# Grouping the block products of a pair by where their weights lie, in a fused attention and channel-mix kernel

## The chip, the cores and the metric

The kernel runs on one core of a Trainium2 chip. The metric is the device time of one execution in microseconds. The kernel before took 392.95 us (median of 3 runs, 392.79 to 394.13).

## What is computed

Input is float32 throughout: 4 sequences of 768 positions, 8 heads of 64. First comes a local attention: chunks of 32 queries see 16 keys to the left, their own 32, 8 to the right and 8 memory keys. Its output, 4 x 768 x 512, is the `x` of a channel mix:

```python
x_prev = concat([zeros, x[:, :-1]], axis=1)
xk = mu_k * x + (1 - mu_k) * x_prev
xr = mu_r * x + (1 - mu_r) * x_prev
k = maximum(xk @ w_k, 0)              # 512 x 1024
v = (k * k) @ w_v                     # 1024 x 512
out = sigmoid(xr @ w_r) * v           # 512 x 512
```

## The kernel before, in words

The 3072 positions are 12 units (u) of 256 positions, each of two tiles (t) of 128. The steps of the program are operations of a small planner (`Plan`), and each has a name:

- `qk{t}`, `vw{t}`: loads of a tile's queries and keys (672 KB) and of its values (512 KB), on SyncE's queue. From unit 4 on the qk loads have two buffers (`ring`); the vw loads have two from unit 3 on.
- `s{u}`: scores of a unit, 128 small matmuls into two PSUM banks (L514). `max`, `sub`, `exp`, `sum`, `norm` follow on VectorE and ScalarE.
- `t{t}`: transposes of a tile's probabilities (L594), copied out of PSUM by `bd{t}.0` and `.1`; `a{t}`: attention product of a tile, 32 small matmuls (L611).
- `g{u}.{c}`: gate block of a tile, 12 matmuls of 512 columns and the last halved (L1104), then `sig` on ScalarE.
- `h{u}.{n}`: hidden blocks. Up to unit 5 there are four a unit, each of 24 matmuls of 256 columns (L1128). `v{u}.{n}`: value blocks; from unit 3 on seven products of 12 matmuls each (`seven`, L1452, banks `pa`, `pb`, `pc`).

Every product of float32 operands is made of three matmuls on split operands (high x high, high x low, low x high). VectorE and ScalarE make these splits.

From unit 6 on two units form a pair (6 and 7, 8 and 9, 10 and 11), and the hidden layer of a pair is computed by `squares` (L883) with seven products in place of eight: products 1 to 7, each in two halves s, so 14 products (q, s) of 12 matmuls of 256 columns (L1060). `PRODUCTS` (L37) gives their order; products 1, 2 and 4 use weights of `w_k` as they are, the others use sums of weights ("forms"). The forms were made once by VectorE, stored to DRAM (`forms`, L803) and are loaded again for each pair into four places (L1026): places 0 and 1 are the second halves of the tiles `wk[0]` and `wk[1]`, places 2 and 3 those of `wv[0]` and `wv[1]` (L795). In the kernel before, product 7.s and 3.s use place s, 6.0 and 6.1 place 2, 5.0 and 5.1 place 3. A place is loaded when the product that used it has ended. The moving operands (b11, b21, b22, t1 to t4 in `with_x`, L939) lie in six places too: two in `xs` (the space of xh0 and xl0), four in `khl`; t1 to t4 are made in place, one from the other. Partial sums go to banks A, G and B for each half; B starts as a copy of A (`seed`), `keep` copies a bank to SBUF, `add` adds a bank to it, `relu` and `sq` end a quarter.

PSUM has eight banks: two for scores, two under the tag `tp` (transposes, attention products), four under `m`, which are given out in turn.

The order of the work: TensorE's is written out by hand in `te_order` (L241). From unit 3 on a unit runs as hidden, attention products, gate, two value products, scores and transposes of a later unit, four value products, gate, last value product. At the end of unit 4 stand `a12 a13 v4.6 t14 t15 s8`, then the four hidden blocks of unit 5. In an even unit from 6 on the 14 products come first, the first gate block before the last of them, then two attention products. The order on the other engines and SyncE's queue is found by the planner: it walks through all operations with modelled costs, takes the one that can start first (`walk`, L140), where an operation with a late due time is put back by at most `WAIT`, and repeats that `PASSES` times with due times taken from the walk before. Each engine then runs its operations in that order.

Of the kernel before, what the change touches and what calls it, by code (L numbers as in the profile page):

```python
# [16 lines left out]
P = 128  # L17
# [17 lines left out]
FAST = 3  # L35
PAIR = 6
PRODUCTS = (  # L37
    (1, 0), (7, 0), (1, 1), (6, 0), (2, 0), (5, 0), (4, 0), (7, 1), (2, 1), (3, 0), (6, 1), (4, 1), (5, 1), (3, 1),
)
# [8 lines left out]
PART = 1.38  # L48
KEEP = ("big", "x4", "vw")
PASSES, WAIT, SLOPE = 40, 0.4, 0.1  # L50
FIRST = """
# [189 lines left out]
def te_order():  # L241
# [4 lines left out]
    for u in range(1, nu):  # L246
        a, b = 2 * u + 2, 2 * u + 3
        g = [("g", u + 1, c) for c in range(QPU) if u + 1 < FAST]
        h = [("h", u, f) for f in range(FT // 2)]
        v = [("v", u, n) for n in range(FT // 2)]  # L250
        x = [("a", a), ("a", b)]
        if u >= FAST:
            g = [("g", u, c) for c in range(QPU)]
            v = [("v", u, n) for n in range(7)]
            t = [("t", a + 2), ("t", b + 2)]
            near = u + 1 if u < PAIR - 1 else u + 2
            x = [("a", near * QPU + c) for c in range(QPU)]
# [36 lines left out]
def local_attention__then__channel_mix(  # L294
# [37 lines left out]
    def ps(tag, name, n=1):  # L332
        return psA.tile([P, n * 512], F32, tag=tag, name=name, bufs=bufs[tag])

# [318 lines left out]
    def mixed(deps):  # L653
        for m in (1, 0):
# [3 lines left out]
            def f_mix(m=m):  # L658
                x = T["xT", 0]
                for i in range(2):  # L660
                    T["xf", 0, m, i] = ps("m", f"xf{m}{i}")
                    for k in range(2 * i, 2 * i + 2):
# [220 lines left out]
    def squares(u0, u1):  # L883
# [38 lines left out]
        def less(name, to, x, y, deps):  # L922
# [15 lines left out]

# [22 lines left out]
        def bank(key, s):  # L961
            T[key, u0, s] = ps(slots[key, s].tag, f"{key}{u0}_{s}")

# [47 lines left out]
        for n, (q, s) in enumerate(PRODUCTS):  # L1011
            key = bank_of[q]
            deps, new, use = [prev], [], []
            if q in (1, 7):
                slots[key, s] = Slot("m" if s == 0 else "tp")
                new = [slots[key, s]]
            if q in direct:
                deps += wdeps(wk_hl, range(direct[q][0], direct[q][0] + 2))
            else:
                j = {7: s, 3: s, 6: 2, 5: 3}[q]  # L1020
                w = Slot(f"wf{j}")
# [9 lines left out]
                use.append(w)  # L1031
            if q == 3 and s == 0:
                operand("b22", "b22", ("x", 0), [mix[u1, 0, 3], t2])
            hh, ll, hs, ls = X[with_x[q]]
# [30 lines left out]
            prev = op(f"h{u0}.{n}", ("pe", PART), f, deps, new=new, use=use, due=due["h", u0, n])  # L1065
            if (q, s) == (5, 1):
                vparts["h"] = prev
            if q not in direct:
                users[j] = prev
            if q == 1:  # L1070
                slots["B", s] = Slot("m")

# [10 lines left out]
            elif q == 6:  # L1083
                done["keep", 5, s] = keep(u0, 2 + s, "B", s, prev)
            elif q == 2:
                relu(u0, s, "A", s, prev)
            elif q == 3:
                relu(u1, s, "B", s, prev)
            elif q == 4:
                add(u0, 2 + s, "G", s, [prev, done["keep", 5, s]])  # L1090
            elif q == 5:
                done["c22", s] = add(u1, 2 + s, "B", s, [prev, done["keep", 4, s]])
        hlast[u0] = hlast[u1] = prev

    def channel_mix(u):
# [45 lines left out]

        def bank(*key):
            T[key] = ps("m", "_".join(str(x) for x in key))

        first = u == 0
        gs = [Slot("m") for _ in range(QPU)]
        sgs = Slot("sg", [0] if u >= PAIR else None)
        xg, xgs = list(mix[u, 1][:2]), list(mix[u, 1][2:])  # L1150
        gdone, prev = [], None
        for n in range(QPU):
            def f_gate(n=n):
                if first:
                    for c in range(QPU):
                        if n == 0:
                            bank("pr", u, c)
                        gate(c, range(n * KT // 2, (n + 1) * KT // 2))
                else:
                    bank("pr", u, n)  # L1160
                    gate(n, range(KT))
# [34 lines left out]
        for n in range(FT // 2):  # L1196
            def f_hidden(n=n):
                if first:
                    for f in range(FT // 2):
                        if n == 0:  # L1200
                            bank("ph", u, f)
                        hidden(f, [n])
                else:
                    bank("ph", u, n)
                    hidden(n, range(KT))
# [54 lines left out]
        for n in range(FT // 2):  # L1260
# [3 lines left out]
            def f_value(n=n, c=c, half=half, fs=fs):  # L1264
                for c in range(QPU) if first else [c]:
                    if n == 0 if first else half == 0:
                        bank("pv", u, c)
                    value(c, fs)
# [26 lines left out]

    sums, free = {}, {}

# [80 lines left out]
    def seven(u, ks, o_g, sgs):  # L1378
# [11 lines left out]
        def operand(name, at, pair, deps):  # L1390
# [16 lines left out]
            ll = op(f"kl{u}.{name}", ("dve", 0.62, True), f_lo, [hh], new=[kl], use=use + [kh])  # L1407
            return hh, ll, kh, kl

# [16 lines left out]
        def bank(key):  # L1426
            T[key, u] = ps("m", f"{key}{u}")

# [70 lines left out]
        last = u == NU - 1  # L1499
        pa, pb, pc = Slot("m"), Slot("m"), Slot("m")  # L1500

# [54 lines left out]
    with tc.manual_schedule():  # L1556
        for o in plan.order(FIRST.split()):
            if o.eng == "pe":
                n = 0 if ("ph", 0, 0) in T else int((o.start - busy - 0.1) / (0.86 if busy else 1.72))
                for _ in range(n):  # L1560
                    warm = warm or ps("m", "warm")
                    nc.tensor.matmul(warm, zero, zeros, start=True, stop=True)
# [51 lines left out]
```

## Time and profile before

| | us |
|---|---|
| median of 3 runs | 392.95 |
| profiled execution | 393.63 |
| its span, first to last instruction | 391.9 |
| TensorE matmuls busy | 382.5 |
| TensorE weight loads busy | 352.9 |
| VectorE busy | 322.3 |
| ScalarE busy | 275.0 |
| GpSimd busy | 14.6 |
| data moved | 63.43 MB, 162 GB/s |

The granted TensorE clock is 1.00 in all forty slices of the span. In the chain of waits a line gives the start, the length and the work, merged (x12: twelve matmuls). Matmuls overlap by far more than their length of 280 ns tells, so the rate is read from the chain or from start to start, not from the busy time. "issue" is time in which an engine waited for nothing that the profile shows.

### The profile page before, as it was taken

To read this page: it belongs to the slowest core of one execution; us is meant where nothing else is said; L and a number is where in the kernel's file an instruction comes from. 1 tells how busy PE (TensorE), PEld (TensorE's weight loads), DVE (VectorE), ACT (ScalarE), POOL (GpSimd) and SP (SyncE) were. 2 spreads that over 40 slices of the span, in tenths; PEclk is the share of its full clock that TensorE was granted. 3 is DMA by queue.
4 is the path that set the end of the run, shared out by engine and by line. 5 is a ranking of instruction groups with operands and counts; after the bars stand their busy time and mean duration, and the time that the engine had idled before them with its cause. 6 is when DMAs were issued, how large, how long until landed. Compare 5 with 4: busy or idle time off the path is not lost.

```text
span 391.9 us, 11008 instructions
## 1 busy us (share of the span) xinstructions
PE 382.5 (98%) x4736; PEld 352.9 (90%) x4736; DVE 322.3 (82%) x540; ACT 275.0 (70%) x466; POOL 14.6 (4%) x14
## 2 busy tenths in 40 slices
PE   7799999999999999999899999999999999999996
PEld 3579889888988999999899999999999999999996
DVE  3699999888898999789979996799996598666673
ACT  3876795914795799488388597678877767496631
POOL 2221003010000000000000000000000000000000
PEclk9999999999999999999999999999999999999999
DMA  8999870411063246464837376735056601160011
GB/s 316 412 371 380 316 286 2 141 55 54 2 212 131 105 148 213 176 202 142 264 134 276 129 230 223 239 121 163 2 165 215 213 2 56 58 204 11 0 55 54
DMA packets 25344, 63.43 MB, mean 162 GB/s; under 512 B 2512, under 2 KB 9040, under 8 KB 24784
## 3 DMA queue, kind: packets, MB, share of 16 engines
q1 hardware_dynamic: 25296, 62.73, 45.4%
q8 instruction: 37, 0.61, 0.6%
q14 instruction: 11, 0.09, 0.1%
HBM read 52.24 MB, written 10.49 MB: 160 GB/s over the span
## 4 chain that ended last, share of the span: by engine, by line
PE 94%; ACT 2%; DVE 2%; DMA 1%; issue 0%
PE pr L1104 17%; PE ph L1128 17%; PE pc L1452 10%; PE pv L1104 8%; PE B L1060 7%; PE pa L1452 6%; PE pb L1452 6%; PE px L611 6%; PE G L1060 4%; PE A L1060 4%; PE s L514 4%; PE pt L594 3%; PE xf L665 2%; ACT k L399 1%; DMA qk<-in_qk_dram 1%
## 5 line engine op out<-in xcount | busy, mean ns | idle before, releaser
L1128 PE MATMUL ph<-xh,wkh 128*128 128x256 f32 x192 | 53.7, 280 | 1.0 <-issue 1.0
L1128 PE MATMUL ph<-xh,wkl 128*128 128x256 f32 x192 | 53.4, 278 | 0.0
L1128 PE MATMUL ph<-xl,wkh 128*128 128x256 f32 x192 | 53.3, 278 | 0.0
L1104 PE MATMUL pr<-wrh,xh 128*128 128x512 f32 x96 | 38.3, 399 | 0.0
L1403 DVE TENSOR_TENSOR khl<-k,khl 128x512 fp32r<-128x512 f32 x42 | 28.9, 688 | 10.7 <-ACT khl L369 10.5
L1104 PE MATMUL pr<-wrl,xh 128*128 128x512 f32 x96 | 37.6, 392 | 0.0
L1104 PE MATMUL pr<-wrh,xl 128*128 128x512 f32 (+1 forms) x117 | 37.6, 351 | 0.0
L1128 PEld LDWEIGHTS ph<-xh,wkh 128*128 128x128 f32 x192 | 36.2, 188 | 1.5 <-issue 1.2
L1128 PEld LDWEIGHTS ph<-xh,wkl 128*128 128x128 f32 x192 | 36.1, 188 | 0.0
L1128 PEld LDWEIGHTS ph<-xl,wkh 128*128 128x128 f32 x192 | 36.0, 188 | 0.0
L369 ACT CAST khl<-k 128x512 fp32r<-128x512 f32 x50 | 30.6, 618 | 3.5 <-DVE k L1413 3.1
L369 ACT COPY aTz<-pt 64x512 f32<-64x512 f32 x45 | 26.0, 580 | 8.0 <-PE pt L594 7.2
L1104 PE MATMUL pv<-wvh,khl 128*128 128x512 f32 (+1 forms) x97 | 30.3, 390 | 0.0
L1452 PE MATMUL pc<-wtbig,khl 128*128 128x256 f32 x216 | 28.2, 280 | 0.0
L1452 PE MATMUL pa<-wvh,khl 128*128 128x256 f32 x144 | 27.9, 279 | 0.0
L1452 PE MATMUL pb<-wtx,khl 128*128 128x256 f32 x216 | 27.5, 276 | 0.0
L611 PEld LDWEIGHTS px<-aTz,vw 128*64 128x64 f32 x768 | 23.4, 138 | 4.1 <-DVE aTz L371 2.6
L1223 ACT ACTIVATE k<-ph 128x512 f32<-128x512 f32 x24 | 14.1, 595 | 18.1 <-PE ph L1128 17.9
L611 PE MATMUL px<-aTz,vw 128*64 128x64 f32 x768 | 25.0, 224 | 1.6 <-DVE aTz L371 1.6
L1104 PEld LDWEIGHTS pr<-wrh,xl 128*128 128x128 f32 x117 | 22.0, 188 | 4.8
L1452 PEld LDWEIGHTS pc<-wtbig,khl 128*128 128x128 f32 x216 | 26.1, 188 | 0.0
L1452 PEld LDWEIGHTS pb<-wtx,khl 128*128 128x128 f32 x216 | 25.9, 188 | 0.0
(169 smaller groups left out, 1004.0 us busy)
## 6 DMA issues: line engine op xcount, KB each, us to landing
vw<-in_vw_dram SPq DMA_DIRECT2D x24, 512.0 KB, 5.4
ring<-in_qk_dram SPq DMA_DIRECT2D x16, 672.0 KB, 5.8
out_dram<-o SPq DMA_DIRECT2D x23, 256.0 KB, 2.1
qk<-in_qk_dram SPq DMA_DIRECT2D x8, 672.0 KB, 6.3
raw<-in_w_k_dram SPq DMA_DIRECT2D x4, 1024.0 KB, 7.8
raw<-in_w_v_dram SPq DMA_DIRECT2D x4, 1024.0 KB, 6.8
wvh<-forms SPq DMA_DIRECT2D x12, 256.0 KB, 3.1
wvl<-forms SPq DMA_DIRECT2D x12, 256.0 KB, 3.3
```

The source lines that it names most:

```text
L369: e.copy(dst, src)
L399: nc.scalar.activation(T["diag", m][:, j, k], id_sb, AF.Copy, scale=mu_sb[:, m + 2 * j, k : k + 1])
L514: nc.tensor.matmul(room(h, c)[CHUNK * j : CHUNK * (j + 1), r, :], q4[z, r, j, :], k3[z, r, STEP * j : STEP * j + NK], start=True, stop=True,)
L594: nc.tensor.transpose(p[:, n * P : (n + 1) * P], e[:, n // 2, c, n % 2, :], id_sb)
L611: nc.tensor.matmul(p3[64 * h : 64 * h + 64, 2 * g : 2 * g + 2, CHUNK * j : CHUNK * j + CHUNK], v[:, g, h, j, :], a[:, h, g, j, :], start=True,
L665: nc.tensor.matmul(z, T["diag", m][:, j, k], x[:, k, 1 - j : 1 - j + UTOK], start=j == 0, stop=j == 1)
L1060: nc.tensor.matmul(z, w, x[:, k], start=q in (1, 7) and i + k + m == 0, stop=i + k == 2 and m == 2, skip_group_check=q not in (1, 7),)
L1104: nc.tensor.matmul(p[:, a : a + step], x, w[:, a : a + step], start=start, stop=stop and a + step == DM)
L1128: nc.tensor.matmul(z, w, x[:, k], start=start, stop=stop)
L1223: e.activation(r, T["ph", u, f], AF.Relu)
L1403: nc.vector.tensor_sub(T["al", u, name], block(at), T["ah", u, name].bitcast(F32))
L1452: nc.tensor.matmul(p, l[:, i], r[i], start=start, stop=stop, skip_group_check=not fresh)
```

## The change

- `PRODUCTS` has a new order, by the tiles that hold the weights: (1, 0), (7, 0), (1, 1), (7, 1) in `wk[0]` and `wk[1]`; (2, s), (4, s) in `wk[2]` and `wk[3]`; (6, s) in places 2 and 3; (5, s) in places 0 and 1; (3, s) in places 2 and 3.
- In `te_order` the two attention products of units 6 and 8 stand on either side of the products 6, and the first gate block between the products 5 and 3. In unit 10, which has no attention, the gate block stands between 5.0 and 5.1, and the second gate block behind two value products.
- The transposes 14 and 15 and scores 8 move from the end of unit 4 into the hidden blocks of unit 5.
- The operands change places: b22 takes the `khl` place of t1 and is split before t2 is made; t2 overwrites b22's block; t4 is made from b21 and t2; t1 is split late, into b11's place. `add` for product 4's bank comes after product 6.
- In `seven` only a22 waits for the end of the pair's hidden products (all 14 now, before up to (5, 1)); the other operands wait for the last split of the same place.
- PSUM banks `m` get places: the planner picks the one that is free first (`KEEP`), and from unit 5 on most are fixed.
- The loads `qk{t}` and `vw{t}` from tile 12 on wait for a later step of TensorE. `WAIT` goes from 0.4 to 0.6, `SLOPE` from 0.1 to 0.15.

```diff
 PRODUCTS = (
-    (1, 0), (7, 0), (1, 1), (6, 0), (2, 0), (5, 0), (4, 0), (7, 1), (2, 1), (3, 0), (6, 1), (4, 1), (5, 1), (3, 1),
+    (1, 0), (7, 0), (1, 1), (7, 1), (2, 0), (2, 1), (4, 0), (4, 1), (6, 0), (6, 1), (5, 0), (5, 1), (3, 0), (3, 1),
 )
-KEEP = ("big", "x4", "vw")
-PASSES, WAIT, SLOPE = 40, 0.4, 0.1
+KEEP = ("big", "x4", "vw", "m")
+PASSES, WAIT, SLOPE = 40, 0.6, 0.15
...
+            if u == PAIR - 1:
+                h = h[:1] + extra[2:] + h[1:3] + extra[:2] + h[3:]
...
                 if u == PAIR - 2:
-                    seq += [("a", n + QPU) for _, n in x] + v[6:] + [("t", n + QPU) for _, n in t] + [("s", near + 3)]
+                    extra = [("t", n + QPU) for _, n in t] + [("s", near + 3)]
+                    seq += [("a", n + QPU) for _, n in x] + v[6:]
...
-                seq += h[:-1] + g[:1] + h[-1:] + x
                 if u == nu - 2:
-                    seq += g[1:] + v
+                    seq += h[:11] + g[:1] + h[11:] + v[:2] + g[1:] + v[2:]
                     continue
+                seq += h[:8] + x[:1] + h[8:10] + x[1:] + h[10:12] + g[:1] + h[12:]
...
+        pv = vparts[u0 - 1]
...
-        l21 = operand("b21", "b21", ("k", 0), [mix[u0, 0, 3], vparts[u0 - 1][5]])
-        lt1 = operand("t1", "b11", ("k", 2), [t1, vparts[u0 - 1][6], vparts[u0 - 1][3]])
-        t2 = less("t2", "b11", "b22", "b11", [lt1, t3])
-        operand("t2", "b11", ("k", 3), [t2, vparts[u0 - 1][3]])
-        t4 = less("t4", "b21", "b21", "b11", [t2, l21])
-        operand("t4", "b21", ("k", 1), [t4, vparts[u0 - 1][6]])
+        l21 = operand("b21", "b21", ("k", 0), [mix[u0, 0, 3], pv[5]])
+        l22 = operand("b22", "b22", ("k", 2), [mix[u1, 0, 3], pv[3], pv[6]])
+        t2 = less("t2", "b22", "b22", "b11", [l22, t3])
+        t4 = less("t4", "b21", "b21", "b22", [t2, l21])
+        operand("t4", "b21", ("k", 1), [t4, pv[6]])
+        operand("t2", "b22", ("k", 3), [t2, pv[3]])
...
-                slots[key, s] = Slot("m" if s == 0 else "tp")
+                slots[key, s] = Slot("tp") if q == 1 else Slot("m", [s])
...
-                j = {7: s, 3: s, 6: 2, 5: 3}[q]
+                j = s if q in (5, 7) else 2 + s
...
-                operand("b22", "b22", ("x", 0), [mix[u1, 0, 3], t2])
+            if q == 5 and s == 0:
+                operand("t1", "b11", ("x", 0), [t2])
...
-                slots["B", s] = Slot("m")
+                slots["B", s] = Slot("m", [3 - s])
...
-        gs = [Slot("m") for _ in range(QPU)]
+        gs = [Slot("m", None if u < PAIR else [int(u < NU - 2)] if n == 0 and (u - PAIR) % 2 == 0 else [3]) for n in range(QPU)]
...
-                free[u] = [vparts["h"]]
+                free[u] = [hlast[u]]
...
-            deps = deps + free.get(u, [])
+            if name == "a22":
+                deps = deps + free.get(u, [])
+            deps = deps + behind.get(pair, [])
...
-        pa, pb, pc = Slot("m"), Slot("m"), Slot("m")
+        pa, pb, pc = (Slot("m", [n] if u >= PAIR - 1 else None) for n in range(3))
...
+    line = sorted((o for o in plan.ops if o.alts[0][0] == "pe"), key=lambda o: o.due)
+    at = {o.name: n for n, o in enumerate(line)}
+    for o in plan.ops:
+        if o.name[:2] in ("qk", "vw") and int(o.name[2:]) // QPU > FAST + 2:
+            t = int(o.name[2:])
+            n = at[f"s{t // QPU - 1}"] + 5 if o.name[0] == "q" else at[f"a{t - 2}"] + 2
+            o.deps.append(line[n])
```

## Rows read from the trace of the kernel before

**Rows 1.** The page: busy time; instruction queue (packets, MB, share); engines of the chain.
```profile
PE 382.5 (98%) x4736; PEld 352.9 (90%) x4736; DVE 322.3 (82%) x540; ACT 275.0 (70%) x466; POOL 14.6 (4%) x14
...
q8 instruction: 37, 0.61, 0.6%
...
PE 94%; ACT 2%; DVE 2%; DMA 1%; issue 0%
```

**Rows 2.** TensorE's waits: engine, line, releaser; us in total, times, longest.
```profile
PE px L611 <- DVE aTz L371: 1.6, 2, 0.8
...
PE ph L1128 <- issue: 1.0, 1, 1.0
PE B L1060 <- DVE khl L915: 0.2, 1, 0.2
```

**Rows 3.** The chain in order of time, hidden blocks: start us, us, what.
```profile
125.64 11.09 PE ph L1128 x96
...
156.51 10.88 PE ph L1128 x96
...
190.26 1.42 PE s L514 x89
191.67 1.57 PE ph L1128 x12
193.25 1.00 issue
194.25 10.16 PE ph L1128 x84
```

**Rows 4.** The chain, pair of units 8 and 9.
```profile
283.96 1.36 PE A L1060 x12
...
288.04 1.42 PE B L1060 x12
...
302.08 2.73 PE pr L1104 x13
304.81 1.38 PE B L1060 x12
306.19 2.02 PE px L611 x64
308.20 1.58 PE pa L1452 x12
...
311.15 0.87 PE pt L594 x8
```

**Rows 5.** Windows on four value products, units 8 and 6, matmuls alone.
```profile
312.02:317.68 5.66, 5.66 (x48) 5.45 (x47) 1.00 0.07 27
254.60:260.07 5.47, 5.47 (x48) 5.27 (x47) 1.00 0.60 224
```

**Rows 6.** Windows: the pairs' stretches, products alone; the first number is the length.
```profile
283.96:309.78 25.82, 19.66 (x168) 19.38 (x167) 1.00 0.62 190
224.14:250.80 26.66, 20.23 (x168) 19.52 (x167) 1.00 0.66 212
339.09:361.31 22.22, 19.66 (x168) 19.38 (x167) 1.00 0.35 119
```

**Rows 7.** Timeline of unit 6: the second wait within its products.
```profile
241.38 0.30 PEld L1060 LDWEIGHTS B<-khl,wvh 128*128 128x128 f32 x2 [0.23 <-ACT k L369]
```

**Rows 8.** Timeline of SyncE's queue: the vw loads behind attention product 8.
```profile
137.86 1.69 SPq L587 DMA_DIRECT2D vw<-in_vw_dram  x2
```

**Rows 9.** The page's DMA issues: the last number is us from issue to landing.
```profile
ring<-in_qk_dram SPq DMA_DIRECT2D x16, 672.0 KB, 5.8
```

**Rows 10.** The page's costliest groups: VectorE's low part of a value operand.
```profile
L1403 DVE TENSOR_TENSOR khl<-k,khl 128x512 fp32r<-128x512 f32 x42 | 28.9, 688 | 10.7 <-ACT khl L369 10.5
```

**Rows 11.** Instructions on tile aTz: the copies of transposes, ns min/median/max.
```profile
L369 ACT COPY aTz<-pt x45: 558/580/587, 14.7 to 313.9; 64x512 f32<-64x512 f32 x45
```

**Rows 12.** Waits of SyncE's queue: the stored forms.
```profile
SPq L852 <- DVE ring L371: 12.0, 3, 4.8
```

More of the change, by code (lines that the diff above doesn't have):

```diff
@@ L332, in ps @@
     def ps(tag, name, n=1):
-        return psA.tile([P, n * 512], F32, tag=tag, name=name, bufs=bufs[tag])
+        if isinstance(tag, Slot):
+            tag = f"{tag.tag}at{tag.place}" if tag.tag == "m" else tag.tag
+        return psA.tile([P, n * 512], F32, tag=tag, name=name, bufs=bufs.get(tag, 1))
     id_sb = const.tile([P, P], F32, tag="ident", name="id_sb")
@@ L660, in f_mix @@
                 for i in range(2):
-                    T["xf", 0, m, i] = ps("m", f"xf{m}{i}")
+                    T["xf", 0, m, i] = ps(ss[i], f"xf{m}{i}")
                     for k in range(2 * i, 2 * i + 2):
@@ L961, in bank @@
         def bank(key, s):
-            T[key, u0, s] = ps(slots[key, s].tag, f"{key}{u0}_{s}")
+            T[key, u0, s] = ps(slots[key, s], f"{key}{u0}_{s}")
         def keep(u, f, key, s, dep):
@@ L1031, in squares @@
                 use.append(w)
-            if q == 3 and s == 0:
-                operand("b22", "b22", ("x", 0), [mix[u1, 0, 3], t2])
+            if q == 5 and s == 0:
+                operand("t1", "b11", ("x", 0), [t2])
             hh, ll, hs, ls = X[with_x[q]]
@@ L1065, in squares @@
             prev = op(f"h{u0}.{n}", ("pe", PART), f, deps, new=new, use=use, due=due["h", u0, n])
-            if (q, s) == (5, 1):
-                vparts["h"] = prev
             if q not in direct:
@@ L1084, in squares @@
                 done["keep", 5, s] = keep(u0, 2 + s, "B", s, prev)
+                add(u0, 2 + s, "G", s, [done["keep", 5, s], done["p4", s]])
             elif q == 2:
@@ L1089, in squares @@
             elif q == 4:
-                add(u0, 2 + s, "G", s, [prev, done["keep", 5, s]])
+                done["p4", s] = prev
             elif q == 5:
@@ L1140, in value, with bank @@
                         product(p, x[:, tc_], w, f + n == 0, stop, stop and c == QPU - 1 and u == 1)
-        def bank(*key):
-            T[key] = ps("m", "_".join(str(x) for x in key))
+        def bank(slot, *key):
+            T[key] = ps(slot, "_".join(str(x) for x in key))
         first = u == 0
-        gs = [Slot("m") for _ in range(QPU)]
+        gs = [Slot("m", None if u < PAIR else [int(u < NU - 2)] if n == 0 and (u - PAIR) % 2 == 0 else [3]) for n in range(QPU)]
         sgs = Slot("sg", [0] if u >= PAIR else None)
@@ L1156, in f_gate @@
                         if n == 0:
-                            bank("pr", u, c)
+                            bank(gs[c], "pr", u, c)
                         gate(c, range(n * KT // 2, (n + 1) * KT // 2))
                 else:
-                    bank("pr", u, n)
+                    bank(gs[n], "pr", u, n)
                     gate(n, range(KT))
@@ L1200, in f_hidden @@
                         if n == 0:
-                            bank("ph", u, f)
+                            bank(ms[f], "ph", u, f)
                         hidden(f, [n])
                 else:
-                    bank("ph", u, n)
+                    bank(ms[n], "ph", u, n)
                     hidden(n, range(KT))
@@ L1266, in f_value @@
                     if n == 0 if first else half == 0:
-                        bank("pv", u, c)
+                        bank(vs[c], "pv", u, c)
                     value(c, fs)
@@ L1294, in channel_mix @@
             op(f"out{u}.{c}", ("dma", 0.65), f_st, [o_o], use=[os], due=dv + BLOCK + 6)
-    sums, free = {}, {}
+    sums, free, behind = {}, {}, {}
     def quarter(s, kh, nh):
@@ L1403, in f_lo @@
                 nc.vector.tensor_sub(T["al", u, name], block(at), T["ah", u, name].bitcast(F32))
-            deps = deps + free.get(u, [])
+            if name == "a22":
+                deps = deps + free.get(u, [])
+            deps = deps + behind.get(pair, [])
             hh = op(f"kh{u}.{name}", either(act=(0.6,), dve=(0.36, True)), f_hi, deps, new=[kh], use=use)
             ll = op(f"kl{u}.{name}", ("dve", 0.62, True), f_lo, [hh], new=[kl], use=use + [kh])
+            behind[pair] = [ll]
             return hh, ll, kh, kl
@@ L1426, in bank @@
         def bank(key):
-            T[key, u] = ps("m", f"{key}{u}")
+            T[key, u] = ps({"pa": pa, "pb": pb, "pc": pc}[key], f"{key}{u}")
         def half(key):
@@ L1560, in local_attention__then__channel_mix @@
                 for _ in range(n):
-                    warm = warm or ps("m", "warm")
+                    warm = warm or ps("mat0", "warm")
                     nc.tensor.matmul(warm, zero, zeros, start=True, stop=True)
```

## The prediction

> **What bounds the kernel now.** I read the page first, then who waited for whom, then the chain of work in order of time, then windows on single stretches. The page says that TensorE is the limit: 98% busy and 94% of the chain that ended last [rows 1]. The list of TensorE's waits holds 6.0 us in all, most of it in the first 30 us, which the change doesn't touch; three of its lines matter here [rows 2]. So a gain must come from TensorE's own time: from a wait in mid-kernel, from the rate at which it takes matmuls, or from the price of switching between kinds of work. All three are seen in the chain.
>
> First, a hole. In unit 5 the four hidden blocks take 1.57 + 1.00 + 10.16 = 12.73 us, with 1.00 us in which TensorE waited for nothing that the profile shows; elsewhere four such blocks take 10.88 (units 2 to 4: 11.09 right behind a scores block) [rows 3]. The hole comes in the midst of a block, just behind a scores block, whose 128 matmuls and 128 weight loads run through in 1.42 us. The instruction queue moved 0.61 MB in 37 packets [rows 1]; over 2 x 4736 TensorE instructions that is 64 B each and 256 instructions a packet, so that one scores block uses up a whole packet in 1.42 us. I read the hole as code that came late. That is argued, since no view names it.
>
> Second, two rates. Twelve matmuls of 256 columns take 1.36 us or 1.41 us. In the pair of units 8 and 9 the first products take 1.36, the fourth 1.42 [rows 4], and the fourteen together 19.49 where 13 at 1.36 and the one behind the gate at 1.38 would make 19.06 (worked out below). It isn't the clock and isn't traffic: the same four value products took 5.66 us at a DMA share of 0.07 and 5.47 us at a share of 0.60, both at clock 1.00 [rows 5]. The slow rate begins where the stationary weights pass from the wk tiles to the wv tiles, and it stays until a gate block or a further such passage ends it; behind a gate block it was the fast rate each time.
>
> Third, attention products. Two in a row take 2.02 us, and the product behind them 1.58 in place of 1.36 [rows 4]: 1.01 us each, and 0.22 us for the turn.
>
> **The change, part by part.** The times are sums for the profiled execution (393.63 us, of them 391.9 us span).
>
> *Unit 5.* The transposes of tiles 14 and 15 and scores 8 go from in front of the hidden blocks to between them: block, scores 8, two blocks, transposes, block. The work is the same. The blocks are then 10.88 plus two restarts, each of 0.21 (11.09 against 10.88, rows 3): 11.30 us against 12.73, so **-1.43 us**, of which 1.00 is the hole. It should not come back behind scores 8, because now 24 matmuls stand before and 48 behind it, where two attention products, two transposes and the scores block came within six microseconds. If the last block runs at the slow rate, 0.1 of it is lost.
>
> *Pair of units 8 and 9.* New order: products 1.0, 7.0, 1.1, 7.1, 2.0, 2.1, 4.0, 4.1 (weights in wk), attention product, 6.0, 6.1 (wv), attention product, 5.0, 5.1 (wk), gate, 3.0, 3.1 (wv). Now every passage between wk and wv has other work in it. If that keeps the fast rate: 13 x 1.36 + 1.38 behind the gate = 19.06 us; gate 2.73; two single attention products, each 1.01 + 0.22, 2.46; the first value product 1.36. Sum 25.61 against 25.82 [rows 6]: **-0.21 us**. The rate alone gives 0.43 (the products were 25.82 - 2.73 - 2.02 - 1.58 = 19.49), and the second turn takes 0.22 back.
>
> *Pair 6 and 7.* The same stretch took 26.66 [rows 6], that is 0.84 more than the pair behind it. It waits 0.2 us for t2's low part (VectorE, rows 2) and 0.23 us for the copy of B on ScalarE [rows 7]; each wait also costs a restart. t2 is now wanted at the ninth product, not the fourth; the copy, which stood on ScalarE behind a relu that waits for the last stored forms, now comes before that relu. Both waits should go, and the forms are wanted no earlier, 7.1 excepted, whose place is free from the end of unit 5. What is late next is t4 at the seventh product, as late as before and then without a wait. 26.66 - 25.61 = **-1.05 us**.
>
> *Pair 10 and 11* has no attention, and 6.0 follows 4.1 directly: three products at 1.41 and, from 3.0 on, two more, so 21.79 + 0.25 = 22.04 against 22.22 [rows 6]: **-0.18 us** (between 0 and -0.43).
>
> These four give -2.87 us. Against them stand waits that before does not show:
>
> *Held-back loads.* From tile 12 on, a qk load waits for the fifth TensorE step behind the last scores, a vw load for the second step behind the attention product that freed its buffer; both were issued as soon as the buffer was free. Nothing else waits behind them but SyncE's queue (stores, forms). Tight is scores 6: its loads now start with the end of attention product 8, where SyncE issues the vw loads today [rows 8], and are wanted 6.7 us later (1.01 + 0.22 + 2.73 + 2 x 1.36), the second tile 0.7 after that. A qk load takes 5.8 us (median) [rows 9], the second is issued some 0.6 later. From 0 up to the issue of two vw loads that might go first, 1.7 us [rows 8]; a gain is out, since an earlier load never stopped TensorE. I take 0.1, nearest the median. All other held-back loads have over a microsecond to spare.
>
> *The operand a22* may be split only after product 3.1, no longer after 5.1, and s2 needs it. In unit 8 two value products and two transposes (1.36 + 1.36 + 0.87 = 3.59 us, rows 4) stand between; five VectorE passes at up to 0.69 [rows 10] make 3.45. From 0 to 1.2 (a longer VectorE pass that gets in between); I take 0.1.
>
> *Transposes 14 and 15* now lie one block (2.72 us) before their attention products: four copies of 0.58 on ScalarE [rows 11], 2.3 us. From 0 to 0.8, the longest such wait now [rows 2]: 0.05.
>
> *Restarts behind a single attention product* might land in the slow rate: two groups in each of two pairs, 0.1 each: from 0 to 0.4; I take 0.1. On the other side the four slow products of unit 8 [rows 5] may turn fast: down to -0.2, taken as nothing.
>
> *PSUM places* are fixed and loads on VectorE and ScalarE stay what they were: no instruction more. The gate's bank is wanted again 4 us behind it, its sigmoid takes 0.6: nothing.
>
> That is +0.35, and the net -2.5 us: 391.1 for the profiled execution. The three runs have a median of 392.95, 0.68 under it; the same step from there gives **390.4 us**.
>
> **The rivals.**
>
> *A. The hole is not in every execution, or moves behind another scores block.* For it: no view names its cause, and the three runs lie 1.34 us apart, about the hole and its restart. Against it: it stands where code is used fastest. Then 1.2 of the 1.43 is not won: 391.6 us.
>
> *B. Places don't matter.* The slow rate is something into which any restart can fall, and the new passages keep it: the products stay at 19.49, and the second turn of attention costs its 0.22 for nothing. For it: 5.66 and 5.47 us for the same operands [rows 5]; against it: all three pairs slow down at the same product. 0.43 + 0.43 + 0.18 less won: 391.4 us. The Trainium skill is on this side: "TensorE: Matmul & The Clock Gate" (Step-by-step) says that loading the next weights takes no read bandwidth from the running matmul; by that rule, where the two lie can't cost anything, and no row here shows it as a rule.
>
> *C. Slower: held-back loads come late.* The mechanism is SyncE's in-order queue. The loads for scores 9 may be issued only at the end of unit 5's last hidden block, 7.7 us before they are wanted (two attention products with their turn, a gate, two value products), at the moment that also frees the first form loads. If a stored form stands in front of them and waits for VectorE (one did for up to 4.8 us [rows 12]), the 1.7 us that they have to spare (7.7 less 5.8 and the issue) are used up and 3.1 missing, with up to 1.7 more at scores 6: 390.4 + 4.8 = 395.2 us. It decides from 2.5 us of late loading on. Against it: their buffers leave them the rest of the time idle, and the due times put a load that is wanted next in front.
>
> **How the numbers follow.** Forecast 0.55 (389.5 to 391.4, with its unknown costs at either end), A 0.18, B 0.12, C 0.15. What this kernel's runs can tell from no change is about 0.5%, 2 us: under 391.0 or over 394.9. Under 391.0 lie three quarters of the forecast and a sixth of A and B: 0.46. Over 394.9 lie two thirds of C: 0.10. The rest, 0.44, is between. With A and B inside, and outside two thirds of C and what of the forecast's unknown costs comes out better than their lower ends, the range is 389.4 to 394.2.
>
> **What would show it.** Right: no idle microsecond in unit 5, and its four blocks at some 11.3 us; the first eight products of each pair at 1.36; the pairs 6 and 8 equally long. A: 1 us of "issue" at another scores block. B: products 2.0 to 4.1 at 1.41. C: TensorE waiting for qk or vw under scores 6 or 9. The prediction is wrong if the pairs keep their length, or if TensorE waits for an operand that it didn't wait for before.

## The result and the profile after

The changed kernel takes 399.39 us (median of 6 runs, 398.05 to 399.7) against 393.68 us for the kernel before on the same chip: a ratio of **1.0136, 95% interval 1.0111 to 1.0162. It is 1.4% slower**; forecast was 390.4 us, and the range ended at 394.2.

The profiled execution (398.05 us, span 396.3, mean granted clock 0.996) is the shortest of the six; the other five take 398.63 to 399.7 us at a mean clock of 0.991. Its page answers to [rows 1]. TensorE has the same number of matmuls (4736). In the chain that ended last its share is 5 points lower, and those of VectorE and DMA are 2 points higher each:

```profile
PE 89%; DVE 4%; DMA 3%; ACT 2%; issue 0%; SPq 0%; DVEq 0%
```

TensorE's waits in the changed kernel, in the columns of [rows 2], have a new first line, and the idle "issue" in front of a hidden block is gone:

```profile
PE xf L670 <- DVE xl L684: 4.6, 1, 4.6
```

The timeline says where that is (start us, length, engine, line, operation, idle time before it and its releaser). `xf` are unit 0's two mixes of 16 matmuls each; between them TensorE stands still until VectorE has read the first:

```profile
19.33 3.69 PE L670 MATMUL xf<-xTs,k 128*128 128x256 f32 x16
27.61 5.41 PE L670 MATMUL xf<-xTs,k 128*128 128x256 f32 x16 [4.59 <-DVE xl L684]
```

In the kernel before, the same 32 matmuls stand in one piece, and the first hidden block follows at 31.28 us:

```profile
18.99 7.07 PE L665 MATMUL xf<-xTs,k 128*128 128x256 f32 x32
...
31.28 0.39 PE L1128 MATMUL ph<-xh,wkh 128*128 128x256 f32 x1
```

In the changed kernel the second 16 matmuls also take longer than the first 16. Windows on the first mix, the wait, the second mix and what follows give the granted clock in the third number from the end:

```profile
19.33:23.02 3.69, 3.69 (x16) 2.91 (x16) 3.56 (x4) 2.88 (x4) 1.08 (x1) 1.00 1.00 414
23.02:27.61 4.59, 0.00 (x1) 0.01 (x1) 4.52 (x8) 1.62 (x3) 0.00 (x0) 1.00 1.00 405
27.61:32.85 5.24, 5.24 (x16) 4.27 (x17) 0.54 (x1) 0.59 (x1) 0.00 (x0) 0.67 0.69 227
32.85:37.85 5.00, 4.61 (x201) 4.05 (x199) 2.73 (x4) 4.08 (x8) 2.36 (x1) 1.00 0.32 112
```

Right behind the idle stretch the clock is 0.67 on average, a stretch at the lower of its two levels (1.2 GHz in place of 2.4) and then full again. The first hidden block starts 37.85 us into the span. Against 31.28 that is +6.57 us, while from there to the end the changed kernel takes 358.45 us against 360.62: **-2.17 us**. So the middle of the kernel gained about what was forecast (-2.5), and the start lost three times as much.

The gain in the middle, in the chain of the changed kernel. Unit 5, which answers to [rows 3], has no idle time in it:

```profile
195.91 2.72 PE ph L1133 x24
198.63 1.41 PE s L519 x89
200.04 5.66 PE ph L1133 x48
...
206.58 2.83 PE ph L1133 x24
```

And the pair of units 8 and 9, which answers to [rows 4]:

```profile
288.22 1.36 PE A L1066 x12
...
293.66 2.72 PE A L1066 x24
296.38 2.72 PE G L1066 x24
299.10 1.08 PE px L616 x32
300.18 2.94 PE B L1066 x24
...
307.12 2.74 PE pr L1109 x13
309.87 2.83 PE B L1066 x24
312.69 1.41 PE pa L1460 x12
```

The first eight products go at 1.36 us each, as forecast (x24 are two products). The two behind the gate block take 2.83 together, the slow rate, and the value products pa and pb behind them 1.41 each, so that the stretch through pa takes 25.88 us against 25.82 [rows 6].

### The profile page after: what moved, and what is told of

Same layout as the page of the kernel before. It is cut to its first block, busy times and chain, and to the rows that moved or that the text cites. A ratio compares the mean times of both kernels' runs of the same rounds, so it can differ in the third digit from the quotient of the medians.

```text
span 396.3 us, 11022 instructions
## 1 busy us (share of the span) xinstructions
PE 383.5 (97%) x4736; PEld 353.0 (89%) x4736; DVE 323.9 (82%) x547; ACT 270.9 (68%) x459; POOL 15.8 (4%) x15
## 4 chain that ended last, share of the span: by engine, by line
PE 89%; DVE 4%; DMA 3%; ACT 2%; issue 0%; SPq 0%; DVEq 0%
PE pr L1109 17%; PE ph L1133 15%; PE pc L1460 9%; PE pv L1109 8%; PE B L1066 7%; PE pa L1460 6%; PE pb L1460 6%; PE px L616 5%; PE G L1066 4%; PE A L1066 4%; PE s L519 4%; PE pt L599 3%; DMA vw<-in_vw_dram 2%; PE xf L670 1%; ACT k L404 1%; DMA qk<-in_qk_dram 1%
## 5 line engine op out<-in xcount | busy, mean ns | idle before, releaser
L374 ACT CAST khl<-k 128x512 fp32r<-128x512 f32 x45 | 27.9, 620 | 2.3 <-PE B L1066 0.9
```

The lines of the kernel that those rows point to most:

```text
L374: e.copy(dst, src)
```

## The experiments

**The wait between the mixes.** The changed `mixed()` asks for its banks by the planner's places, inside a function that runs only when the plan is written out. `ss` is set anew by each pass of the loop over the two mixes, so both functions see the list of the last pass: two banks for both mixes, where the planner had laid out four. x1 binds the list when the function is made:

```diff
-            def f_mix(m=m):
+            def f_mix(m=m, ss=ss):
```

> The changed kernel with one word more: f_mix binds its own pair of PSUM banks, as it binds m. In the changed kernel the name ss is looked up when the step is written out, after the loop, so both mixes of unit 0 go to the banks of the last one; the planner meant four. Theory 1 (the whole loss is that shared pair): TensorE no longer waits 4.6 us between the two mixes, the clock stays at 1.00, and the gains of the middle remain: span 389.5 to 390.2, ratio to before 0.993 to 0.996. Rival (the start is late for another reason: the new waits, WAIT and SLOPE, or the loads): the first hidden block of unit 0 still starts at about 38 us and the ratio stays at 1.01 or more.

392.16 us (12 runs, 391.56 to 393.13): ratio to before **0.9955 [0.9939, 0.9971]**, faster than both kernels, by little against before and clear of the noise. The timeline of x1 has the 32 matmuls in one piece, and its first hidden block starts at 31.65 us:

```profile
19.66 7.14 PE L670 MATMUL xf<-xTs,k 128*128 128x256 f32 x32
```

On every engine the order of the instructions is that of the changed kernel, so the 7.2 us between the two are the banks alone.

x2 was to show the same from the other side: before, with the second mix written over the first in the very same tile (`T["xf", 0, 0, i]`), so that the first mix's result is left out.

> The kernel before, and only this: the second mix of unit 0 takes the two PSUM banks of the first, where before it took two of its own. Theory 1: TensorE waits 4 to 5 us between the mixes, the clock falls to half for some 3.4 us behind it, the first hidden block starts at 37 to 39 us in place of 31.3, and the kernel takes 399 to 401 us (ratio 1.014 to 1.020). Rival (the shared banks alone cost little, since weights set the start): under 1.005.

396.21 us, ratio 1.0073 [1.0038, 1.0108], under the 399 to 401 us expected, and with the 32 matmuls in one piece again: the second mix went ahead of the first one's readers. What it lost stood elsewhere: TensorE waited 2.38 us for `aTz` (3.3 us in all), and behind that wait the 64 matmuls of an attention product took 3.52 us in place of 2.08, at a mean clock of 0.54. It made no such wait as the one in question, so it tells nothing about that.

x5 splits the 7.2 us. It is the changed kernel, with both mixes still in the same two banks and five 512-column products of zeros between them (two matmuls each in the trace), in a bank that is not in use yet:

```diff
-            def f_mix(m=m):
+            def f_mix(m=m, own=ss):
...
+                if m == 1:
+                    w = ps(own[0], "warm2")
+                    for _ in range(5):
+                        nc.tensor.matmul(w, zero, zeros, start=True, stop=True)
```

> The changed kernel as it is, both mixes of unit 0 still in the same two banks, with five 512-column products of zeros put on TensorE between the two mixes, into a bank that is not yet in use. In the trace of before, and of the changed kernel, such a product takes about 0.86 us at full clock, so the five take about 4.3 us and lie inside the wait of 4.59 us. It separates the two parts of the 7.2 us by which the changed kernel (399.4 us) is longer than the one with the banks bound (392.2). Theory: the wait costs 4.6 us, and the idle TensorE then costs its clock, the other 2.6 us. Then the wait stays (the stage of the mixes still about 11.5 us), the granted clock stays 1.00 and the time is about 396.8 us, ratio to before about 1.007. Rival 1: the clock falls for another reason, or the 2.6 us are elsewhere: the time stays at 399 us. Rival 2: the wait is not the cause: the products of zeros are added on top, 403 us.

397.04 us (396.52 to 397.51), ratio 1.0079 [1.0051, 1.0108]. The timeline and the windows of x5, of the same three stretches:

```profile
23.07 4.46 PE L668 MATMUL warm<-zero_sb 128*128 128x512 f32 x10
27.82 3.72 PE L674 MATMUL xf<-xTs,k 128*128 128x256 f32 x16 [0.29 <-DVE xl L688]
```
```profile
23.07:27.82 4.75, 4.46 (x12) 1.72 (x10) 4.68 (x8) 1.77 (x3) 0.00 (x0) 1.00 1.00 405
27.82:31.37 3.55, 3.55 (x16) 3.08 (x17) 0.54 (x1) 0.58 (x1) 0.00 (x0) 1.00 0.87 307
```

With TensorE kept at work the wait costs its own length and no more: the second mix takes 3.55 us at clock 1.00, in place of 5.24 at 0.67. Of the 7.2 us between the medians, 2.4 are the clock (399.39 - 397.04) and 4.9 the wait (397.04 - 392.16, of which 4.75 show here). In the second mix itself the clock cost 1.7 us (5.24 - 3.55), near the 1.5 us between the two profiled executions (398.05 - 396.58); where the other five executions of the changed kernel lost their further clock isn't shown.

**The idle stretch of unit 5.** The prediction gave 1.43 us to spreading the transposes and scores 8 over the hidden blocks. x3 is before with that part alone; x14 is x3 profiled once more, x13 before once more.

```diff
...
+            if u == PAIR - 1:
+                h = h[:1] + extra[2:] + h[1:3] + extra[:2] + h[3:]
```

> The kernel before, and only the spread of extra attention: transposes 14 and 15 and scores 8 stand within unit 5's hidden blocks. By my step for unit 5: no idle microsecond there, its stretch 1.4 to 1.6 us shorter, ratio 0.996 to 0.997. Rival A (the hole comes with code that is late somewhere else, or with the loads that are issued as before): the hole stands behind scores 8 or 9 still, ratio 0.999 to 1.001.

> The kernel before, unaltered, profiled once more. Theory (the idle stretch of 1.0 us behind scores 8 belongs to the program and its early loads): idle time of 0.8 to 1.3 us behind scores 8 again, unit 5's hidden blocks about 12.7 us. Rival A of the prediction (it is not in every execution): no idle stretch there, the hidden blocks at 11.1 us.

> Before with only the spread of transposes 14, 15 and scores 8 over unit 5, profiled once more. In its first profile the idle stretch had not gone but stood in scores 8 (2.95 us instead of 1.42), and from unit 5's value product to its gate block the stretch was 18.63 us, as in before. Theory (the spread alone moves the stall and doesn't remove it): 18.3 to 18.7 us again, with idle time in or beside scores 8. Rival (the stall comes and goes with the execution, which would fit the 0.35 % by which this kernel is shorter than before): 17.1 us and no idle time.

x3 takes 392.88 us, ratio 0.9965 [0.9944, 0.9986], the size expected, but its chain refutes the reason. The idle time stands within scores 8 now:

```profile
189.86 2.72 PE ph L1131 x24
192.58 1.38 PE s L517 x87
193.96 1.26 issue
195.22 0.30 PE s L517 x4
```

In x14 (392.40 us) it is 0.18 us at the same spot. x13 (395.83 us) has it where before had it, twice as long, and it costs the clock as well: chain, then windows on the idle stretch and the blocks behind it.

```profile
191.74 1.57 PE ph L1128 x12
193.31 2.10 issue
195.41 11.41 PE ph L1128 x84
```
```profile
194.00:196.90 2.90, 1.49 (x12) 1.49 (x13) 2.83 (x5) 0.00 (x0) 0.00 (x0) 1.00 0.98 369
196.90:201.22 4.32, 4.32 (x26) 4.32 (x25) 1.13 (x3) 3.57 (x4) 0.00 (x0) 0.61 0.42 162
```

All these stops are in one place, if one counts instructions instead of naming them. In before and x13, 8 transposes, 128 matmuls of scores and 12 of a hidden block come between the value product pc and the stop; in x3 and x14, 24 of a hidden block and 124 of scores: 148 each time. Counted from the start of each trace, the stop is ahead of TensorE's matmul 2643 (2642 in x2, which has it too). It doesn't belong to an operation, then, but to a point in TensorE's stream of instructions, and the spread only moved other work there. From pc to unit 5's gate block the stretch takes 18.63 us in before, 20.98 in x13, 18.63 in x3 and 17.54 in x14: how long the stop is differs from execution to execution, so that x3's shorter median may come from shorter stops; one profile a kernel doesn't tell.

What took it away in the changed kernel, then? x4 is x1 without the held-back loads (`o.deps.append(line[n])` left out); x6 and x10 are x1 with the transposes and scores 8 put back together, x10 with the qk loads held back to three steps behind the scores in place of five; x11 is before with the held-back loads alone (three steps).

> The changed kernel with its banks bound (as x1) and without the later start of the qk and vw loads: each is issued when its buffer is free. If the later loads are what removes the hole in unit 5, TensorE idles about 1 us behind a scores block in units 5 to 7 and this is 0.8 to 1.3 us slower than x1. If order alone removes it: within 0.4 us of x1.

> The kernel with the banks bound (392.2 us), with the transposes of attention 14 and 15 and scores 8 put back together in front of unit 5's hidden blocks, and the held-back loads kept. Theory (spreading them is worth what the prediction gave it, 1.4 us): the idle stretch of about 1 us behind scores 8 returns with its restarts, 393.3 to 393.7 us, ratio to the kernel with the banks bound about 1.0035. Rival: the idle stretch came from loads that the holding back has moved anyway; no idle time there, only restarts, 392.2 to 392.5 us.

> The kernel with the banks bound, with transposes 14 and 15 and scores 8 together in front of unit 5's hidden blocks, and the loads of q and k held back to three operations behind the scores before instead of five. Without that, the last batch showed no idle stretch at scores 8 (hidden blocks of unit 5 at 11.09 us), but the loads for scores 9 were issued 1.8 us later, landed about 6 us later, and scores 9 with the value product before them took 1.6 us more. Theory (once loads are held back the spread is worth nothing by itself, both undo the same stall): no wait at scores 9 and none at scores 8, the time of the kernel with the banks bound, 392.2 us, within 0.3. Rival (the spread is worth its 1.4 us also then): 393.5 us, with idle time behind scores 8 or restarts in unit 5 that add up to over 1 us.

> The kernel before, with nothing of the change but the held-back loads of q, k and v (q and k three operations behind the scores before). The prediction gave the held-back loads a cost of 0.1 us. Theory (the idle stretch behind scores 8 comes from loads that land on it, so that holding them back undoes it, as the spread did): no idle stretch of 1 us in front of unit 5's hidden blocks, which take about 11.1 us; the time 1.2 to 1.4 us below before, ratio 0.9965. Rival A (the idle stretch comes from the order of the instructions alone): the stretch is still there, ratio 0.999 to 1.001. Rival B (held-back loads come too late in the old order): a wait for a load in front of scores 9 or later, ratio above 1.001.

x4: 393.50 us, ratio 0.9994 [0.9975, 1.0013], 1.3 us above x1. The stop is back at matmul 2643, in scores 8 (chain), and a value product waits 0.4 us for ScalarE. In the profiled execution the stop with its restart is worth 0.47 us of the 1.3 (scores 8 take 1.88 us against 1.41 in x1):

```profile
193.66 0.20 issue
193.86 0.30 PE s L519 x4
```

x10: 391.74 us, ratio 0.9957 [0.9940, 0.9974], no slower than x1 without any spread, and no idle time in unit 5. x6: 392.96 us, 0.9975 [0.9954, 0.9995], has none there either; it lost at scores 9, whose loads SyncE issued from 202.69 us on (200.87 in x1); the second landed 9.55 us after its issue, and TensorE waited 1.2 us. The chain of x10, then that of x6, which passes through the load:

```profile
191.69 11.09 PE ph L1133 x96
```
```profile
191.82 10.43 PE ph L1133 x90
...
202.69 0.42 SPq L480
...
203.17 9.55 DMA ring<-in_qk_dram
```

x11: 393.18 us, 0.9979 [0.9964, 0.9995]; its stop is still at matmul 2643 but shorter, and no slow rate follows it:

```profile
193.37 0.41 issue
193.78 9.69 PE ph L1128 x84
```

So the spread alone doesn't remove the stop, and with held-back loads it adds nothing. The six profiles with early loads (before, x2, x3, x4, x13, x14) stop there; of the ten with held-back loads only x11 does.

What TensorE waits for there can be read from the same traces. One packet of the instruction queue holds 256 instructions [rows 1], and the DMA view shows when a packet moves if its window is narrowed down. In before, the packet in question lies in the window 191.8:192.9, in front of the stop that ends at 194.25:

```profile
q8 instruction: 1, 0.02, 5.5%
```

In the nine traces without the stop this packet starts within 0.6 us of matmul 2498 (1.10 us in x12; x5 is counted without its products of zeros); in the seven with it, only 1.65 to 3.60 us after that matmul, the latest in x13, which stops longest. In each of the seven, the stopped matmul starts 1.21 to 1.53 us after the packet has landed; in the nine, the same matmul comes 1.54 us (x12) to 2.45 us after the landing. Early in the kernel all sixteen traces have a stop of the same kind: ahead of matmul 224 TensorE idles 0.39 to 1.74 us on "issue", and goes on 1.25 to 1.56 us after a code packet has landed. So the stop is code that came late.

What makes it late is seen on SyncE's queue, in the times at which the vw loads are issued. Before, then x1, then x10 (matmul 2498 is at 189.55, 189.79 and 189.56 us):

```profile
186.91 1.26 SPq L587 DMA_DIRECT2D vw<-in_vw_dram  x2
```
```profile
187.15 0.33 SPq L592 DMA_DIRECT2D vw<-in_vw_dram  x1
```
```profile
189.17 1.80 SPq L592 DMA_DIRECT2D vw<-in_vw_dram  x2
```

In all seven traces that stop, two vw loads were issued 2.5 to 2.7 us and 1.6 to 1.7 us before matmul 2498, and both were still on their way at that matmul. In six of the nine others one had been issued, and the second comes 1.7 us or more behind that matmul; in x6, x10 and x12 both are issued only from 0.4 us before it on. x11 holds its loads back too, but in the order of before its two vw loads go at the same place (187.02 us, matmul 2498 at 189.67). The qk loads can't have delayed the packet in x3 and x4, where they are issued 3.4 us behind matmul 2498; that it is the vw loads is read from these times, since no run holds them back alone. x12 shows how near a stop can be: its packet starts 1.10 us behind that matmul and lands just in time. That the stop is gone holds for the executions that were profiled.

**The pauses in a pair.** Three orders of x1's pairs 6/7 and 8/9: x7 has both attention products behind everything, x8 exchanges the gate block and the second attention product, x9 joins both attention products in the place of the first.

```
x1  h[:8] + x[:1] + h[8:10] + x[1:] + h[10:12] + g[:1] + h[12:]
x7  h[:12] + g[:1] + h[12:] + x
x8  h[:8] + x[:1] + h[8:10] + g[:1] + h[10:12] + x[1:] + h[12:]
x9  h[:8] + x + h[8:12] + g[:1] + h[12:]
```

> The kernel with the banks bound (392.2 us), with the two attention products of a pair again one behind the other, behind all fourteen products and the gate block, in pairs 6/7 and 8/9; the products stay grouped by the place of their weights. Theory A (breaking the row of products restores the fast rate of 113.3 ns for a matmul, which is what the separate attention products were for): products 6 and 5 (48 matmuls a pair) go at 117.7 ns, 0.21 us a pair more, while the joined attention products cost 2.02 us instead of 2 times 1.28, 0.54 less; both pairs together 0.65 us shorter, 391.5 us. Theory B (the order itself of the pauses is free): the products stay at 113.3 ns and the joined ones win the whole 0.54 a pair, 391.1 us. Theory C (the single ones hide something, as the conversions of products 5 or 3 that are late when no attention stands before them): new waits before products 6, 5 or 3, 392.5 to 394 us.

> The kernel with the banks bound (392.2 us), with the gate block and the second attention product of pairs 6/7 and 8/9 exchanged: the gate block stands in front of products 5, in a bank of the attention's, and the attention product in front of products 3. It is to tell what the slow rate hangs on that begins behind the gate block there (117.7 ns for a matmul in products 3 and on into the value products pa and pb, 48 matmuls). Theory A (a gate block leaves the slow rate, an attention product takes it away): products 5 at 117.7 ns, products 3, pa and pb at 113.3; 0.1 us a pair shorter, 392.0 us, not to be told by the time but by the spacing of the matmuls. Theory B (it hangs on products 3 or their operands): products 5 stay at 113.3 ns, products 3 at 117.7; 392.2 us. Theory C: the bank of the attention's is not free in time, and the gate block waits: slower by up to 1 us a pair, with a wait in front of the gate block.

> The kernel with the banks bound, with both attention products of pairs 6/7 and 8/9 joined between products 4 and 6 (the place of the first of them now), the gate block where it is. The last batch showed: joined behind all products, products 6 and 5 go at 117.7 ns from the first matmul of 6; a single attention product costs 1.28 us with what it drains, the joined pair about 2.1. Theory A (the step from products 4 to products 6 brings the slow rate, and one attention product there takes it away for 6 and 5 both, so the second is a pure cost): 6 and 5 at 113.3 ns, products 3 behind the gate at 117.7; through pa a pair takes 25.88 less 0.45, about 25.4 us, both pairs together 0.9 us shorter than with the banks bound, 391.3 us. Theory B (the second attention product is what keeps products 5 fast): 5 at 117.7 ns, 0.1 us a pair more than A, 391.5 us. Rival: products 6, 5 or 3 wait for a conversion that the second attention product gave time to: a wait in front of them, 392 us or more.

x7 391.57 us (0.9947 [0.9928, 0.9967]), x8 392.15 (0.9956 [0.9938, 0.9974]), x9 391.61 (0.9955 [0.9938, 0.9972]): the times don't part them, the chains do. Pair 8/9 from product 6.0 on in x7, then in x8 from products 5 on, then in x9 from 6.0 on:

```profile
292.56 5.66 PE B L1066 x48
298.21 2.77 PE pr L1109 x13
300.99 2.82 PE B L1066 x24
```
```profile
300.29 2.74 PE B L1066 x24
303.03 1.08 PE px L616 x32
304.11 2.94 PE B L1066 x24
307.05 1.41 PE pa L1460 x12
```
```profile
294.50 5.77 PE B L1066 x48
...
303.02 2.83 PE B L1066 x24
```

In x7 products 6 and 5 are slow throughout (48 x 117.8 ns = 5.66): theory A. In x8 products 5 stay fast behind the gate (24 x 113.3 + 0.02) and products 3 behind attention too (2.72 + 0.22), but pa is slow: neither theory whole. In x9 the starts of the matmuls lie 113 ns apart in products 6 and 118 in products 5: 48 x 113.3 + 0.22 + 24 x 4.4 ns = 5.77, theory B. So in x7 and x9 the slow rate begins at a direct passage between wk places and wv places, where x1, with an attention product there, stays fast. More than that these traces don't make a rule of. In before a further passage ended the slow rate (product 5.0 in pair 10/11, first fence below). A gate block is followed by the fast rate (x8's products 5; before, the last product [rows 4]) or by the slow one (products 3 in x1, x7 and x9), and the place of the weights doesn't decide it alone: in the changed kernel the value product pc, whose weights lie in wv as well, turns fast behind unit 8's second gate block, after a slow pa (second fence). Why pa turns slow behind fast products 3 in x8 stays open too.

```profile
346.00 1.38 PE B L1060 x12
```
```profile
320.63 1.41 PE pa L1460 x12
...
324.82 1.38 PE pc L1460 x12
```

**The two improvements together.** x12 is x10 with x9's order.

> The kernel with the banks bound, with both of the last edits at once: the two attention products of a pair joined between products 4 and 6, and transposes 14 and 15 and scores 8 left in front of unit 5's hidden blocks with the loads of q and k held back three operations behind the scores. By themselves they gave spans of 389.4 and 389.7 us against 390.0 with the banks bound. Theory (they touch different stretches and add): a span of about 389.1 us and a time of 391.0 to 391.4 us, ratio to before about 0.994. Rival (the loads held back three operations behind the scores land on other work when the pairs are shorter): a wait at scores 9 or 10, no better than 391.6 us.

391.27 us (391.02 to 392.34), 0.9950 [0.9935, 0.9966]: the shortest median and span (389.3 us), at the upper part of what was expected, and not to be told from x7, x9 or x10 by its interval.

## Why the prediction was wrong

**The step that failed is the last of its additions:** "*PSUM places* are fixed and loads on VectorE and ScalarE stay what they were: no instruction more ... nothing", with the sentence ahead of it that most of TensorE's waits lie "in the first 30 us, which the change doesn't touch". The change touches them in one line of `mixed()`, where the bank's name went from a rotating tag to a place read from `ss`. That is not an instruction more, but two banks fewer. The second mix had to wait for the slowest reader of the first, VectorE's `xl`, which stands behind the softmax and the decoding of weights in VectorE's order and starts at 26.87 us, hidden before because the mixes had banks of their own. Price: 4.9 us of wait and 2.4 of clock between the medians. None of the rivals was this one: only of the gate's bank did the prediction ask when it is wanted again. One of its signs of being wrong came, though, since TensorE waits for an operand that it didn't wait for before.

**Unit 5 (-1.43):** the stretch from pc to the gate block went from 18.63 to 17.08 us, -1.55: the size came out, and the edit was the wrong one. That the size came out is in part luck, since the stop of before was 1.00 us in the profile that the sum used and 2.10 in x13. Reading the idle stretch as late code held up: the packet is in the traces. Concluding that the stop "should not come back behind scores 8" because other work stands before did not hold, since what counts is the number of instructions and when the packet of the next ones arrives. x3 has rival A in it: the stop moved into scores 8 itself, and it is shorter or longer in each execution.

**Held-back loads (+0.1, "a gain is out"):** mis-signed. The second vw load, held back, is what let the code packet through, and in x4 against x1 the held-back loads are worth 1.3 us. The bounds excluded a gain because no earlier load had made TensorE wait for data; but the early vw load had made it wait for code, and the trace of before shows it (packet 2.31 us behind matmul 2498). Scores 6 and 9, which rival C feared for, waited for nothing. x6 shows what C feared, a wait of 1.2 us at scores 9, from loads issued 1.8 us later that took up to 9.55 us to land; two loads of forms stand in front of them in SyncE's queue, not a stored form that waits, as C had it.

**Pair 6/7 (-1.05), 8/9 (-0.21), 10/11 (-0.18):** measured -0.77 (25.89 against 26.66), +0.06 and -0.11 (22.11 against 22.22, products and gate). Both waits of pair 6/7 went, and the two pairs are equally long, as forecast. Each pair is 0.27 us above the 25.61 that was worked out: two single attention products cost 2.58 with their turns, not 2.46 (+0.12); products 3 took 2.83, not 2.74 (+0.09); pa 1.41, not 1.36 (+0.05). The second and third are the claim that a gate block always leaves the fast rate; among the products of a pair it rested on gates with wk weights behind them.

**Rival B** is refuted: products 1, 7, 2 and 4 went at 1.36 once their weights lay in one place, and in x7 and x9 the slow rate starts at the passage. What the prediction drew from the Trainium skill, "TensorE: Matmul & The Clock Gate" (Step-by-step), that a weight load which takes no read bandwidth from a running matmul can't make places matter, doesn't hold here: 113.3 against 117.7 ns for the same matmul at clock 1.00. Whether the weight loads are what costs the 4.4 ns, no run here shows.

Without the fault of the banks the forecast would have been near: it gave a ratio of 390.4/392.95 = 0.9935, and x1 has 0.9955 [0.9939, 0.9971], though in unit 5 by the vw load and not by the spread.

## What to carry to other kernels

When a diff changes how a buffer is named, follow the name to each allocation and ask how many distinct buffers come out, above all where code runs later than the loop that made it: no list of instructions shows it, and one row of the waits does. When TensorE idles on "issue", count instructions up to the stop in two orders of the program: if the count stays and the operation changes, moving work won't help. Find the code packet that landed last before TensorE went on, and the loads issued ahead of it; holding one of these back can be the whole gain. Price an idle stretch of TensorE with what its clock does behind it.

## What was not expected of the hardware

- 4.59 us without a matmul brought the clock to 0.67 over the next 5.24 us, 2.38 us (x2) to 0.54 over the next 3.45 us, and 2.10 us (x13) to 0.61 in a stretch of 4.32 us that began 1.5 us behind it. 1.00 us in before left it at 1.00, as did the 4.75 us of x5 that were filled with products of zeros.
- One point of the instruction stream (matmul 2643) stopped TensorE for 0.18 to 2.10 us in seven profiles of five programs, with different operations on either side of it. In each it went on 1.21 to 1.53 us after a code packet of 16 KB had landed, and in each two data loads of 512 KB were on their way when the packet was due.
- The same matmul of 256 columns starts every 113.3 or every 117.7 ns at clock 1.00. Which of the two it is changes with the tile that holds the weights and with the work in between: behind attention products (32 or 64 small matmuls) it was the fast one each time here, behind a gate block only sometimes.
